# Third weight column rounded later, T1 in place of B12 in the classical columns, and another product order in the first Strassen pair

## The chip, the core and the metric

The kernel runs on one core of one Trainium2 chip. The metric is the device time of one execution in microseconds (us), as the median of several runs.

## What is computed

The reference is soft-capped attention followed by a mixture-of-experts style MLP with squared ReLU.

```
scores = cap * tanh(q @ k^T / sqrt(64) / cap);  attn = softmax(scores);  a = attn @ v
x = a, laid out as 1792 tokens x 768
h = maximum(x @ w_in, 0)          # w_in 768 x 2048
out = (h * h) @ w_out             # w_out 2048 x 768
```

There are 4 batches with 12 heads of 448 x 64. The weights come as 64-bit floats. TensorE multiplies rounded operands, and each operand is split into a high and a low part, so that a product of two matrices is three matmuls for each block (high x high, high x low, low x high).

## The kernel before

**Attention.** The main loop (from L615) runs over n, 24 pairs of heads, with two stages in flight: an iteration makes the scores of pair n on TensorE (PE, `scores` L410) and multiplies probabilities and v for pair n-1 (`pv_half` L454, `pv` L465, `sums` L472). ScalarE (ACT) does tanh and exp (L428, L436). VectorE (DVE) adds probabilities (L440, L445), inverts the sums of an older pair (L485), transposes the next k and q (L401), normalises an older pair into x (L509) and, last, empties the accumulators of pair n-1 from PSUM (`evac`, L478). In every iteration `evac` of pair n-1 has to be done before `pv_half` of pair n may write to the accumulators, since there is one such tile.

**Work slipped into attention.** Tables indexed by n put preparation for the MLP between these instructions. A weight column is 128 columns of w_in. Rounding it takes "size" (ACT, L40), "rest" (ACT, L43), "clip" (DVE L41), "shift" (L44), "sign" (L46) and "total" (L48). It is then split into high and low for each of its two halves (L572 and L574). `split_x_of` splits half of one 128-row block of x (L519, L520).

**First product.** x is cut into four blocks B11, B21, B12, B22 and w_in into 16 columns f. Columns 0 and 1 are computed classically, in half-products that accumulate two of the blocks each. The other 14 columns are seven pairs p, each a Strassen-Winograd scheme of seven products, numbered (m, p). A product is two halves j = 0, 1 of nine matmuls of 128 x 448 (`product`, L359). Both halves stand in one PSUM tile `hps` of shape [P, 2, 512], one bank per half. The products of a pair share tiles: product 6 adds into the tile seeded by product 1, is copied out as u (`keep_u`, L993, one ACT copy per half), and product 7 goes on adding into the same tile.

**Who sets the order.** In attention the order of each engine is that of the code. Behind it, a planner (`Plan`) holds tasks with costs, due times and dependencies and writes an order for every engine; PE follows the list `seq`. Waits between instructions are kept per tile, so a reader of a tile waits for its last writer.

**After the first product.** The squares are multiplied with w_out by another scheme (L1167), with operands that ACT and DVE split in time.

Of the kernel before, what the change touches and what calls it, by code (L numbers as in the profile page):

```python
# [240 lines left out]
def tile_softcap_attention_mlp(ctx, tc, q, k, v, cap, w_in, w_out, out):  # L241
# [359 lines left out]
    T1 = {24: ((0, 0), (1, 0), (2, 0)), 25: ((0, 1), (1, 1))}  # L601

# [5 lines left out]

    def half_unit(out, f, j, o):
        product(out, ops[f, o], xs[("B11", "B21")[o]], j, o == 0, o == 1)  # L610

# [3 lines left out]
    for n in range(NP + 1):  # L615
# [32 lines left out]
        if n == 1:  # L648
# [3 lines left out]
            nc.vector.memset(guard[top, 1:2], 0.0)  # L652
        if n - 6 in whole:
            split_x_of(n - 6)
# [27 lines left out]
    vector_work(NP + 1)  # L682
    half_unit(first[:, 0], 0, 0, 1)
    make_identity(nc, ident)
# [18 lines left out]
    plan = Plan(  # L703
        raw=[(0.0, i, p) for i, p in ((1, left), (2, right))],
        f=[(0.0, 0, left), (0.0, 1, right), (0.0, 3, right)],
        op=[], r=[(0.0, i) for i in range(2)], u=[(15.0, i) for i in range(3)],
        xf=[], xab=[], a=[(0.0, i) for i in range(NRAW)], ps=[(0.0, i) for i in range(2)],
        x=[(0.0, 0)],
    )

    def taken(room, *token):
        return SimpleNamespace(take=room, token=(0.0, *token))
# [6 lines left out]

    seq = [("u", 0, None), ("u", 1, None), ("u", 0, 0), ("u", 1, 0), (1, 1), ("u", 0, 1), (2, 1), ("u", 1, 1)]  # L720
    NEARLY = len(seq)
    for p in range(1, NFP):
        if p + 1 < NFP:
            seq += [(2, p)] * (p > 1) + [(m, p) for m in (6, 5, 7)] + [(1, p + 1), (4, p), (3, p)]
        else:
            seq += [(m, p) for m in (6, 5, 7, 2, 4, 3)]
    due, END = {}, 4.0
    for x in seq:
        due[x] = END
        END += STEP * (4 if x == seq[1] else 2)  # L730

# [32 lines left out]
    do("PE", 4.0, lambda: None, lag=0.0, due=-1.0)  # L764
    do("DVE", 4.4, lambda: None, lag=0.0, due=-1.0)
    spread_a = do("POOL", 0.7, lambda: spread(NP - 2), ready=5.5, lag=6.5)
# [56 lines left out]
    def round_column(first, f, at, early, raw=None):  # L823
# [12 lines left out]
        if raw:  # L836
            h.fetch, here = taken("raw", 0, left), None
        else:
            h.fetch, here = transfer("SP", fetch, 768, normal[2], due=at - 16.0, ready=at - early, take="raw")
# [26 lines left out]

    left_ops = {(1, "A11"): ready_op(2, 0), (1, "A12"): ready_op(2, 1)}
    columns = {(1, 0): SimpleNamespace(f=held[2], size=taken("f", 2, left), done=None)}
    raw3 = raws[3]

# [4 lines left out]
    def other_ops(p):  # L875
# [3 lines left out]
        at = due[6, p]  # L879
        o = left_ops[p, "A22"] = split_w(a22, at - 1.0, k.done)  # L880
        s1 = do("DVE", 0.56, lambda: nc.vector.tensor_add(out=a22(), in0=a21(), in1=a22()), k.done, o.lo, due=at - 4.0)
        s3 = less(a21, a11, a21, at - 3.5, s1, h.done)
# [17 lines left out]

    columns[1, 1] = round_column(True, 3, due[6, 1] - 5.0, 40.0, raw3)
    for p in range(1, NFP):
# [10 lines left out]
    x11, x21, x12, x22 = ([partial(x_of, a, b, c) for c in range(NHALF)] for a, b in ((0, 0), (0, 1), (1, 0), (1, 1)))  # L913
    at = due["u", 0, 0]
    d12 = [split_x("B12", c, [wide(x12[c])], at, [()], xg[2]) for c in range(NHALF)]
    d22 = [split_x("B22", c, [wide(x22[c])], due["u", 0, 1], [(normal[c],)], xg[0]) for c in range(NHALF)]
    at = due[6, 1] - 9.0
    t1 = [None] * (NHALF - 1) + [do("DVE", 0.62, lambda: t1_part(NHALF - 1, 1), due=at)]
    t3 = [minus(at + c + 0.4, x12[c], x22[c], x12[c], t1[c], *d12[c], normal[c]) for c in range(NHALF)]
    t2 = [minus(at + c + 0.7, x22[c], x22[c], x11[c], t3[c], *d22[c]) for c in range(NHALF)]  # L920
# [16 lines left out]

    def unit_task(key, j):

        _, f, o = key  # L940
        half = o is not None
        parts = [(("B12", "B22")[o], o)] if half else [("B11", 0), ("B21", 1)]

        def emit():
            if j == 0 and not o:
                new_bank("u", f, half)
            for b, k in parts:
                product(banks["u", f, half][:, j], ops[f, k], xs[b], j, k == 0, k == 1)

        need = [t for b, _ in parts for t in has_b[b][j]]  # L950
        return pe(key, emit, *need, cost=STEP * len(parts), take="ps" if j == 0 and not o else None)

# [57 lines left out]

    banks["u", 0, False] = first
    unit_ts = {}
    for key in seq[:NEARLY]:
        if key[0] != "u":
            strassen(*key)
            continue
        _, f, o = key
        ts = unit_ts[key] = [None if key == seq[0] and j == 0 else unit_task(key, j) for j in range(2)]
        half = o is not None
        if o != 0:  # L1020
            opens = unit_ts["u", f, 0 if half else None][0]
            out_u = relu_out(f, int(half), lambda f=f, half=half: banks["u", f, half], due[key], *ts)
            when(out_u, give=[opens or taken("ps", 2)])
        if half:
            when(ts[1], give=[ready_op(f, o).hi])
        if key == ("u", 1, 0):
            b12_read = ts
    d2 = [split_x("T2", c, [wide(x22[c])], due[6, 1] + 0.5 * c, [(t2[c],)], xg[1]) for c in range(NHALF)]
    d1 = [split_x("T1", c, [wide(x11[c])], due[5, 1] + 0.5 * c, [(t1[c], *b12_read)], xg[2]) for c in range(NHALF)]
    for c in range(NHALF):  # L1030
# [304 lines left out]
```

## Time and profile before

| quantity | value |
|---|---|
| median of 3 runs | 580.69 us (579.95 to 581.25) |
| the profiled execution itself | 580.98 us |
| its span, first to last instruction | 579.4 us |
| PE busy | 570.1 us, 98% of the span |
| DVE busy | 468.1 us, 81% |
| ACT busy | 374.7 us, 65% |
| granted TensorE clock | 1.00 of full speed |

A busy time is the union of an engine's instructions. Shares are averages over stages with different limits, so a stage has to be looked at by itself.

### The profile page before, as it was taken

What the parts mean: (1) busy time and instruction counts of PE and PEld (TensorE: products, weight loads), DVE (VectorE), ACT (ScalarE), POOL (GpSimd) and SP (SyncE); (2) the same over time, 40 slices, a digit from 0 to 9 for tenths busy, and PEclk for the clock granted to TensorE, in tenths of its full rate; (3) what the DMA queues carried; (4) which work ended last, traced back from release to release, by engine and by line L of the source; (5) the groups of instructions that cost most, each with busy time, mean ns of one, the idle gap of its engine ahead of it and who ended that gap; (6) DMA issues with size and microseconds to landing.
All of it is one profiled execution on the core that took longest, in us unless ns stands there. A gap on an engine that the chain in (4) does not pass through costs nothing.

```text
span 579.4 us, 10276 instructions
## 1 busy us (share of the span) xinstructions
PE 570.1 (98%) x3862; PEld 454.1 (78%) x3862; DVE 468.1 (81%) x603; ACT 374.7 (65%) x425; POOL 155.2 (27%) x245
## 2 busy tenths in 40 slices
PE   8999999999999999999999999999999999999997
PEld 5333333333369999998999999999999999999996
DVE  3778999999999999788698992756899996766661
ACT  5998999999946878587575873665535633323230
POOL 8788777877221001111120211100000000000000
PEclk9999999999999999999999999999999999999999
DMA  9999999997324837988889878995999236544511
GB/s 132 151 167 170 160 161 170 170 168 144 103 64 127 187 87 242 261 242 237 295 239 297 280 275 305 326 357 192 263 281 291 60 113 210 154 142 144 172 42 44
DMA packets 140728, 110.41 MB, mean 191 GB/s; under 512 B 55456, under 2 KB 129696, under 8 KB 140672
## 3 DMA queue, kind: packets, MB, share of 16 engines
q1 hardware_dynamic: 127136, 72.03, 51.7%
q0 software_dynamic: 12000, 37.39, 23.1%
q8 instruction: 31, 0.51, 0.4%
q10 hardware_dynamic: 1536, 0.27, 0.3%
q14 instruction: 25, 0.20, 0.1%
HBM read 82.84 MB, written 26.65 MB: 189 GB/s over the span
## 4 chain that ended last, share of the span: by engine, by line
PE 68%; issue 13%; DMA 8%; DVE 5%; POOL 3%; ACT 2%; SPq 0%; ACTq 0%; POOLq 0%; DVEq 0%
PE po L1167 35%; PE hps L359 18%; PE pv L465 6%; PE sc L410 5%; DMA kqn<-in_k_dram 2%; PE pv L454 2%; DMA wraw<-in_moe_w_in_dram 2%; DMA w_dram<-wf 1%; POOL kqn L370 1%; POOL g_dram L740 1%; PE pv L472 1%; ACT p L428 1%; PE sc L419 1%; DMA cap_sb<-in_cap_dram 1%; DMA kqn<-in_q_dram 1%
## 5 line engine op out<-in xcount | busy, mean ns | idle before, releaser
L1167 PE MATMUL po<-th,gh 128*128 128x384 f32 x728 | 189.8, 336 | 0.0
L1167 PEld LDWEIGHTS po<-th,gh 128*128 128x128 f32 x728 | 131.9, 188 | 0.0
L1167 PE MATMUL po<-th,gl 128*128 128x384 f32 x392 | 131.7, 336 | 0.0
L1156 ACT CAST gh<-a 128x1024 fp32r<-128x1024 f32 x47 | 49.4, 1051 | 97.5 <-PE po L1167 90.4
L359 PE MATMUL hps<-xt,op 128*128 128x448 f32 x450 | 92.4, 362 | 0.0
L359 PEld LDWEIGHTS hps<-xt,op 128*128 128x128 f32 x450 | 84.4, 187 | 5.6
L428 ACT ACTIVATE p<-sc 128x896 f32<-128x896 f32 x84 | 72.7, 908 | 8.2 <-PE sc L410 6.9
L1167 PEld LDWEIGHTS po<-th,gl 128*128 128x128 f32 x392 | 73.7, 188 | 0.0
L436 ACT ACTIVATE p<-p 128x1792 f32<-128x1792 f32 (+1 forms) x48 | 72.6, 1512 | 1.5
L1157 DVE TENSOR_TENSOR gl<-a,gh 128x1024 fp32r<-128x1024 f32 x47 | 57.5, 1224 | 19.3 <-ACT gh L1156 19.3
L359 PE MATMUL hps<-xs,op 128*128 128x448 f32 x324 | 67.6, 363 | 0.0
L359 PEld LDWEIGHTS hps<-xs,op 128*128 128x128 f32 x324 | 60.6, 187 | 4.7 <-issue 0.4
L370 POOL DMA_DIRECT2D kqn<-in_k_dram x92 | 58.3, 638 | 10.0 <-DVE kq L401 2.2
L410 PE MATMUL sc<-kq 64*64 64x448 f32 x576 | 60.4, 545 | 0.0
L465 PE MATMUL pv<-p,vn 128*32 128x448 f32 x576 | 59.1, 543 | 0.0
L359 PE MATMUL hps<-xh,op 128*128 128x448 f32 x168 | 49.6, 363 | 0.8 <-ACT u L993 0.8
L465 PEld LDWEIGHTS pv<-p,vn 128*32 128x32 f32 x576 | 16.2, 109 | 40.5 <-issue 40.5
L410 PEld LDWEIGHTS sc<-kq 64*64 64x64 f32 x576 | 20.2, 132 | 29.6 <-issue 22.7
L40 ACT ACTIVATE wf<-wraw 128x768 f32<-128x768 f32 x32 | 29.0, 907 | 16.3 <-DMA wraw<-in_moe_w_in_dram 7.8
L387 POOL DMA_DIRECT2D vn<-in_v_dram x48 | 35.2, 738 | 10.6 <-PE pv L465 4.7
L1180 DVE TENSOR_TENSOR osb<-s,po 128x384 f32<-128x384 f32 x27 | 14.9, 553 | 25.9 <-PE po L1167 25.8
L359 PEld LDWEIGHTS hps<-xh,op 128*128 128x128 f32 x168 | 31.5, 187 | 3.1 <-ACT u L993 1.1
(99 smaller groups left out, 807.4 us busy)
## 6 DMA issues: line engine op xcount, KB each, us to landing
a<-g_dram SPq DMA_DIRECT2D x56, 512.0 KB
wraw<-in_moe_w_out_dram SPq DMA_DIRECT2D x16, 768.0 KB
wraw<-in_moe_w_in_dram SPq DMA_DIRECT2D x24, 384.0 KB
g_dram<-r POOLq DMA_DIRECT2D x18, 448.0 KB, 4.5
g_dram<-u POOLq DMA_DIRECT2D x14, 448.0 KB, 4.8
w_dram<-wf POOLq DMA_DIRECT2D x16, 384.0 KB, 6.6
vn<-in_v_dram POOLq DMA_DIRECT2D x48, 112.0 KB, 5.7
kqn<-in_q_dram SPq DMA_DIRECT2D x93, 56.0 KB
```

The source lines that it names most:

```text
L40: size=lambda: nc.scalar.activation(out=magf, in_=high.bitcast(F32), func=ACTF.Abs, scale=2.0 ** 16),
L359: nc.tensor.matmul(out=out, lhsT=w, rhs=x[:, j], start=start and c == 0 and s == 0, stop=stop and c == NHALF - 1 and s == 2, skip_group_ch ...
L370: queue.dma_start(out=kqn[n % NKQ][32 * a:32 * a + 32, i], in_=x)
L387: nc.gpsimd.dma_start(out=vn[n % NKV][r, 1 + i:1 + i + NS], in_=x[i::2].rearrange("t r d -> r t d"))
L410: nc.tensor.matmul(out=sc[out, h, :S], lhsT=kt[r, keys(h, u)][:, out], rhs=qt[r], start=True, stop=True)
L428: nc.scalar.activation(out=p, in_=probs[n, u][:, :, :S], func=ACTF.Tanh, scale=by["qks"])
L436: nc.scalar.activation(out=p, in_=p, func=ACTF.Exp, scale=by["cap"])
L465: nc.tensor.matmul(out=pvs[n][quarter(i), h, :S], lhsT=vn[n % NKV][:, 1 + 3 * h + u, c], rhs=p[:, h], start=False, stop=(u == NU - 1), til ...
L1156: last["act"] = nc.scalar.copy(out=hi, in_=x)
L1157: last["dve"] = nc.vector.tensor_sub(out=lo, in0=x, in1=f32(hi))
L1167: last["mm"] = nc.tensor.matmul(out=po, lhsT=w[:, c], rhs=m[:, cols], start=(c == 0 and i == 0), stop=(c == HF - 1 and i == 2))
L1180: nc.vector.tensor_tensor(out=osb, in0=x, in1=y, op=op)
```

## The change

Three things are edited. The third weight column (f = 2) is not rounded within attention any more: its SCALAR and VECTOR entries are gone, and the planner rounds and splits it in the first product. The splits of x, one per iteration n = 6 to 17 before, stand where a table SPLIT says, and the high and low splits of columns 0 and 1 move to n = 22 and 23. The classical columns take another formula: the top half is B11 A0 + B21 A1 as before, and the bottom half is a copy of B11 A0, plus T1 A0, plus B22 A1, where T1 is a difference that the Strassen pairs need anyway; B12 is not split. The copy is made by ACT from PSUM to PSUM, in two halves, out of the top tile before B21 A1 is added to it. In the first pair, product 5 (which takes T1) goes ahead of 6 and 7.

```
-    SCALAR = {9: (0, "size"), 11: (0, "rest"), 15: (1, "size"), 17: (1, "rest"), 19: (2, "size"), 21: (2, "rest")}
-    VECTOR = {10: ((0, "clip"), (0, "shift")), 12: ((0, "sign"),), 14: ((0, "total"),), 16: ((0, "high0"), (0, "low0")),
-              18: ((0, "high1"), (0, "low1"), (1, "clip"), (1, "shift")), 19: ((1, "sign"),),
-              20: ((1, "total"), (1, "high0"), (1, "low0")), 21: ((1, "high1"), (1, "low1")),
-              22: ((2, "clip"), (2, "shift"), (2, "sign"), (2, "total")),
-              23: ((2, "high0"), (2, "low0"), (2, "high1"), (2, "low1"))}
+    SCALAR = {9: (0, "size"), 11: (0, "rest"), 15: (1, "size"), 17: (1, "rest")}
+    VECTOR = {10: ((0, "clip"), (0, "shift")), 12: ((0, "sign"),), 14: ((0, "total"),), 16: ((1, "clip"), (1, "shift")),
+              18: ((1, "sign"),), 20: ((1, "total"),),
+              22: ((0, "high0"), (0, "low0"), (0, "high1"), (0, "low1"), (1, "high0"), (1, "low0")),
+              23: ((1, "high1"), (1, "low1"))}
+    SPLIT = {6: (0,), 7: (1,), 8: (2,), 9: (3,), 10: (4,), 12: (6,), 14: (8,), 16: (10,), 19: (5,), 21: (7,), 23: (9, 11)}
...
+    UNIT = dict(a=(0, "B11"), b=(1, "B21"), t=(0, "T1"), c=(1, "B22"))
+
+    def half_unit(out, kind, f, j):
+
+        o, b = UNIT[kind]
+        product(out, ops[f, o], xs[b], j, kind == "a", kind in "bc")
...
         if n == NP:
             first = new_ps()
-            half_unit(first[:, 0], 0, 0, 0)
+            second = new_ps()
+            half_unit(first[:, 0], "a", 0, 0)
+            nc.scalar.copy(out=second[:, 0], in_=first[:, 0])
...
-    half_unit(first[:, 0], 0, 0, 1)
+    half_unit(first[:, 1], "a", 0, 1)
+    nc.scalar.copy(out=second[:, 1], in_=first[:, 1])
...
-    seq = [("u", 0, None), ("u", 1, None), ("u", 0, 0), ("u", 1, 0), (1, 1), ("u", 0, 1), (2, 1), ("u", 1, 1)]
+    seq = [("b", 0), ("a", 1), ("b", 1), ("t", 0), ("t", 1), (1, 1), ("c", 0), (2, 1), ("c", 1)]
...
-            seq += [(2, p)] * (p > 1) + [(m, p) for m in (6, 5, 7)] + [(1, p + 1), (4, p), (3, p)]
+            seq += [(2, p)] * (p > 1) + [(m, p) for m in ((5, 6, 7) if p == 1 else (6, 5, 7))] + [(1, p + 1), (4, p), (3, p)]
...
-    columns[1, 1] = round_column(True, 3, due[6, 1] - 5.0, 40.0, raw3)
+    columns[1, 0] = round_column(True, 2, due[1, 1] - 3.0, 40.0, raws[2])
+    for o in range(2):
+        first_op(1, o)
+    columns[1, 1] = round_column(True, 3, due[5, 1] - 3.0, 40.0, raws[3])
...
+        for j in range(2):
+            seeds[f].append(do("ACT", 0.55, partial(seed, j), ts[j], *seeds[f], due=due["b", f],
+                               take=None if j else "ps"))
```

The new line numbers are up to 16 higher than those before: L664 and L690 are the copies for column 0, L951 those for column 1, and L764, L753, L798, L862, L1009 are what L757, L746, L790, L854, L993 were.

**DVE at the end of attention.** These are the rows of the iterations n = 22 and 23 before, each ended by its L478; between them stand the rounding and the splits of column 2.

```order
L445 TENSOR_TENSOR add<-add,p 128x896
L485 RECIPROCAL cmp<-cmp 64x28
L41 TENSOR_SCALAR wf<-wf 128x768
L44 TENSOR_SCALAR wf<-wf 128x768
L46 SCALAR_TENSOR_TENSOR wf<-wraw,wf 128x768
L48 ISA wf<-wraw,wf 128x1536
L509 TENSOR_TENSOR xf<-u 128x448
L478 TENSOR_TENSOR u<-pv,guard 128x896
```

These are the rows of the changed kernel at the same place, from n = 22 on.

```order
L485 RECIPROCAL cmp<-cmp 64x28
L572 CAST op<-wf 128x384
L574 TENSOR_TENSOR op<-wf,op 128x384
...
L509 TENSOR_TENSOR xf<-u 128x448
L478 TENSOR_TENSOR u<-pv,guard 128x896
L440 TENSOR_TENSOR add<-p 128x896
L445 TENSOR_TENSOR add<-add,p 128x896
L485 RECIPROCAL cmp<-cmp 64x28
L519 CAST xs<-xf 128x448
L520 TENSOR_TENSOR xs<-xf,xs 128x448
```

In place of the rounding of column 2 there are three casts and subtractions of columns 0 and 1 in n = 22, and two splits of x and one more cast and subtraction in n = 23.

**ACT between attention and the first product.** Before, ACT ends its softmax work and then makes the casts of x.

```order
L436 ACTIVATE p<-p 128x896 [waits Activation_49]
...
L790 CAST xt<-xf 128x896 [waits PE_49]
L790 CAST xt<-xf 128x896
...
L43 ACTIVATE wraw<-wraw 128x768
L757 ACTIVATE r<-hps 128x896 [waits PE_49]
L746 ACTIVATE r<-r 128x896 [waits Activation_49]
```

In the changed kernel the copies between PSUM tiles stand there.

```order
L664 COPY hps<-hps 128x448 [waits PE_49]
L690 COPY hps<-hps 128x448 [waits PE_49,Activation_49]
...
L798 CAST xt<-xf 128x896 [waits DVE_49] x2
L40 ACTIVATE wf<-wraw 128x768 [waits DMAHW0_49]
L43 ACTIVATE wraw<-wraw 128x768
...
L764 ACTIVATE r<-hps 128x896 [waits PE_49]
L753 ACTIVATE r<-r 128x896 [waits Activation_49]
L951 COPY hps<-hps 128x448 [waits PE_49]
L798 CAST xt<-xf 128x896 [waits DVE_49]
L951 COPY hps<-hps 128x448 [waits PE_49,Activation_49]
```

PE has these rows at the start of the first product of the changed kernel, from the second half of B11 A0 on (hps_1952 is the top tile of column 0, hps_2071 that of column 1; xs_867 opens B21).

```order
L359 MATMUL hps_1952<-xs_632,op_1827 128x448 [waits Activation_49]
L359 MATMUL hps_1952<-xs_632,op_1827 128x448 x2
...
L359 MATMUL hps_1952<-xs_867,op_1830 128x448 [waits Activation_49]
L359 MATMUL hps_1952<-xs_867,op_1830 128x448 x2
...
L359 MATMUL hps_2071<-xs_632,op_1833 128x448 x3
...
L359 MATMUL hps_2071<-xs_786,op_1833 128x448 x3
L359 MATMUL hps_2071<-xs_867,op_1906 128x448 [waits Activation_49]
```

Before, the same products stand there with no wait on ACT. The L690 copy waits for the last matmul of the second half of B11 A0, and the first matmul of B21 A1 waits for it. The first L951 copy waits for the last matmul of the second half too, though it reads the first half, and the second one waits for the first half of B21 A1, which PE writes into the same tile.

**PE and ACT at products 6 and 7 of the first pair.** Before, PE goes from product 6 (tile hps_2244) to 5 (hps_2358) and back to the tile of 6 for product 7.

```order
L359 MATMUL hps_2244<-xt_2227,op_2246 128x448 x3
L359 MATMUL hps_2358<-xt_2212,op_2258 128x448 [waits Activation_49]
L359 MATMUL hps_2358<-xt_2212,op_2258 128x448 [waits DVE_49] x2
...
L359 MATMUL hps_2358<-xt_2215,op_2258 128x448 x3
L359 MATMUL hps_2358<-xt_2260,op_2258 128x448 x3
L359 MATMUL hps_2244<-xh_2292,op_2305 128x448 [waits Activation_49]
L359 MATMUL hps_2244<-xl_2351,op_2305 128x448 [waits DVE_49]
```

In the changed kernel product 5 (hps_2322) is first, and 6 and 7 follow each other in one tile, hps_2237.

```order
L359 MATMUL hps_2322<-xt_2050,op_2287 128x448 x3
L359 MATMUL hps_2237<-xt_2212,op_2283 128x448 x2
...
L359 MATMUL hps_2237<-xt_2250,op_2283 128x448 x3
L359 MATMUL hps_2237<-xt_2253,op_2283 128x448 x3
L359 MATMUL hps_2237<-xh_2235,op_2316 128x448 [waits Activation_49]
L359 MATMUL hps_2237<-xl_2362,op_2316 128x448 [waits DVE_49]
```

The first row of product 7 (operand op_2316) waits for the second of the two copies that ACT makes of product 6, and ACT has these rows there.

```order
L40 ACTIVATE wf_2364<-wraw_2170 128x768
L43 ACTIVATE wraw_2170<-wraw_2170 128x768
L1009 COPY u_2381<-hps_2237 128x448
L798 CAST xh_2385<-xf_895 128x896
L1009 COPY u_2381<-hps_2237 128x448
L798 CAST xh_2393<-u_2366 128x896
```

Product 5's eighteen matmuls no longer lie between the end of product 6 and the start of product 7, and a cast of 896 columns stands between the two copies.

## Rows read from the trace of the kernel before

**Rows 1.** The page, part 1: busy us, share, instructions of each engine.

```profile
PE 570.1 (98%) x3862; PEld 454.1 (78%) x3862; DVE 468.1 (81%) x603; ACT 374.7 (65%) x425; POOL 155.2 (27%) x245
```

**Rows 2.** Busy time of each engine by stretch (--windows; columns named in its head).

```profile
core 0: us, PE busy (x) PEld busy (x) DVE busy (x) ACT busy (x) POOL busy (x), PEclk, DMA share, GB/s
...
15.29:65.85 50.56, 50.56 (x544) 17.78 (x548) 41.84 (x53) 48.19 (x46) 40.21 (x62) 1.00 1.08 161
65.85:157.16 91.31, 90.08 (x957) 30.05 (x949) 87.44 (x121) 88.16 (x85) 66.81 (x102) 1.00 0.92 157
...
166.58:371.00 204.42, 203.64 (x1021) 190.54 (x1018) 174.64 (x250) 144.61 (x204) 33.06 (x55) 1.00 0.77 233
371.00:575.00 204.00, 204.00 (x1178) 203.82 (x1176) 150.48 (x152) 81.91 (x80) 0.54 (x1) 1.00 0.60 183
```

**Rows 3.** Timeline of PE, starts of L454 (n = 11, 23) and of the first product.

```profile
78.66 0.98 PE L454 MATMUL pv<-p,vn 64*64 64x448 f32 x8
...
157.16 0.98 PE L454 MATMUL pv<-p,vn 64*64 64x448 f32 x8 [0.35 <-ACT p L428]
...
166.58 12.88 PE L359 MATMUL hps<-xs,op 128*128 128x448 f32 x63
```

**Rows 4.** Timeline of DVE in attention: a split of x, and one whole iteration.

```profile
107.94 0.34 DVE L519 CAST xs<-xf 128x448 fp32r<-128x448 f32 x1
...
108.86 0.62 DVE L509 TENSOR_TENSOR xf<-u 128x448 f32<-128x448 f32 x1
...
142.70 1.09 DVE L478 TENSOR_TENSOR u<-pv,guard 128x896 f32<-128x896 f32 x1
...
146.14 1.04 DVE L401 STREAM_TRANSPOSE kq<-kqn 128x896 f32<-128x896 f32 x1
147.12 0.31 DVE L572 CAST op<-wf 128x384 fp32r<-128x384 f32 x1
...
147.94 0.62 DVE L509 TENSOR_TENSOR xf<-e 128x448 f32<-128x448 f32 x1
148.66 1.09 DVE L478 TENSOR_TENSOR e<-pv,guard 128x896 f32<-128x896 f32 x1
```

**Rows 5.** Groups of DVE instructions from 76 to 163 us: rounding steps.

```profile
L46 DVE SCALAR_TENSOR_TENSOR wf<-wraw,wf 128x768 uint32<-128x768 uint32 x3 | 2.8, 944 | 0.0
L48 DVE CUSTOM_DVE_ANT_0 wf<-wraw,wf 128x1536 uint16<-128x1536 uint16 x3 | 2.8, 941 | 0.1
...
L44 DVE TENSOR_SCALAR wf<-wf 128x768 uint32<-128x768 uint32 x3 | 1.7, 570 | 0.1
...
L41 DVE TENSOR_SCALAR wf<-wf 128x768 f32<-128x768 f32 x3 | 1.6, 533 | 0.0
```

**Rows 6.** Timeline of PE, then of ACT, around the end of product (6, 1).

```profile
203.89 1.16 PE L359 MATMUL hps<-xt,op 128*128 128x448 f32 x5
...
204.69 0.53 ACT L993 COPY u<-hps 128x448 f32<-128x448 f32 x1 [1.13 <-PE hps L359]
205.12 0.52 ACT L854 CAST op<-wf 128x384 fp32r<-128x384 f32 x1
...
207.64 0.95 ACT L790 CAST xh<-u 128x896 fp32r<-128x896 f32 x1
208.48 0.93 ACT L40 ACTIVATE wf<-wraw 128x768 f32<-128x768 f32 x1
```

**Rows 7.** Timeline of ACT, then of PE, around the one gap of PE.

```profile
265.27 0.89 ACT L40 ACTIVATE wf<-wraw 128x768 f32<-128x768 f32 x1 [2.45 <-DMA wraw<-in_moe_w_in_dram]
266.06 0.52 ACT L993 COPY u<-hps 128x448 f32<-128x448 f32 x1
...
262.09 3.77 PE L359 MATMUL hps<-xs,op 128*128 128x448 f32 x18
266.63 0.47 PE L359 MATMUL hps<-xh,op 128*128 128x448 f32 x1 [0.78 <-ACT u L993]
266.94 0.37 PE L359 MATMUL hps<-xl,op 128*128 128x448 f32 x1
```

More of the change, by code (lines that the diff above doesn't have):

```diff
@@ L652, in tile_softcap_attention_mlp @@
             nc.vector.memset(guard[top, 1:2], 0.0)
-        if n - 6 in whole:
-            split_x_of(n - 6)
+        for m in SPLIT.get(n, ()):
+            split_x_of(m)
         vector_work(n)
@@ L703, in tile_softcap_attention_mlp @@
     plan = Plan(
[L704 to L707, printed above, removed]
+        raw=[(0.0, 2, right)],
+        f=[(0.0, 0, left), (0.0, 1, right), (0.0, 2, left), (0.0, 3, right)],
+        op=[(0.0, i) for i in (4, 5)], r=[(0.0, i) for i in range(2)], u=[(15.0, i) for i in range(3)],
+        xf=[], xab=[], a=[(0.0, i) for i in range(NRAW)], ps=[(0.0, 0)],
         x=[(0.0, 0)],
@@ L729, in tile_softcap_attention_mlp @@
         due[x] = END
[L730 removed]
+        END += STEP * 2
     def transfer(engine, emit, kb, *after, due, give=(), **kw):
@@ L836, in round_column @@
         if raw:
-            h.fetch, here = taken("raw", 0, left), None
+            h.fetch, here = taken("raw", 3 - f, left), None
         else:
@@ L865, in ready_op @@
         return SimpleNamespace(t=ops[f, o], hi=taken("op", 2 * f + o), lo=None)
-    left_ops = {(1, "A11"): ready_op(2, 0), (1, "A12"): ready_op(2, 1)}
-    columns = {(1, 0): SimpleNamespace(f=held[2], size=taken("f", 2, left), done=None)}
-    raw3 = raws[3]
+    left_ops, columns = {}, {}
     def round_pair(p, e):
@@ L936, in new_bank, with seed_second, seed, unit_task @@
         banks[name] = (ps_x.tile([P, 2, 512], F32, tag="x", name="hps")[:, :, :S] if name[0] == "X" else new_ps())
[L938 to L942, printed above, removed]
-        def emit():
[L945 to L951, printed above, removed]
+    seeds = {}
+    def seed_second(f, ts):
+        def seed(j):
+            if j == 0:
+                new_bank("u", f, True)
+            nc.scalar.copy(out=banks["u", f, True][:, j], in_=banks["u", f, False][:, j])
+        seeds[f] = []
+        for j in range(2):
+            seeds[f].append(do("ACT", 0.55, partial(seed, j), ts[j], *seeds[f], due=due["b", f],
+                               take=None if j else "ps"))
+    def unit_task(kind, f, j):
+        b = UNIT[kind][1]
+        def emit():
+            if kind == "a" and j == 0:
+                new_bank("u", f, False)
+            half_unit(banks["u", f, kind in "tc"][:, j], kind, f, j)
+        copied = [seeds[f][j]] if kind in "bt" and f in seeds else []
+        return pe((kind, f), emit, *has_b[b][j], *copied, take="ps" if kind == "a" and j == 0 else None)
     USES = {1: ("A11", "B11", "X"), 2: ("A12", "B21", "X"), 3: ("S4", "B22", "V"), 4: ("A22", "T4", "Y"),
@@ L1009, in strassen @@
                 when(join, give=[bank_by["V", p]])
-    banks["u", 0, False] = first
-    unit_ts = {}
+    banks["u", 0, False], banks["u", 0, True] = first, second
+    bank_by["u", 0, False], bank_by["u", 0, True] = taken("ps", 1), taken("ps", 2)
     for key in seq[:NEARLY]:
-        if key[0] != "u":
+        if key[0] not in UNIT:
             strassen(*key)
             continue
[L1017 to L1021, printed above, removed]
-            out_u = relu_out(f, int(half), lambda f=f, half=half: banks["u", f, half], due[key], *ts)
[L1023 to L1027, printed above, removed]
+        kind, f = key
+        ts = [unit_task(kind, f, j) for j in range(2)]
+        if kind == "a":
+            seed_second(f, ts)
+            bank_by["u", f, False], bank_by["u", f, True] = ts[0], seeds[f][0]
+        if kind in "bc":
+            half = kind == "c"
+            out_u = relu_out(f, int(half), lambda f=f, half=half: banks["u", f, half], due[key], *ts)
+            when(out_u, give=[bank_by["u", f, half]])
+        if kind in "tc":
+            when(ts[1], give=[ready_op(f, UNIT[kind][0]).hi])
     d2 = [split_x("T2", c, [wide(x22[c])], due[6, 1] + 0.5 * c, [(t2[c],)], xg[1]) for c in range(NHALF)]
-    d1 = [split_x("T1", c, [wide(x11[c])], due[5, 1] + 0.5 * c, [(t1[c], *b12_read)], xg[2]) for c in range(NHALF)]
     for c in range(NHALF):
```

19 lines of the change are left out of this document (8 added, 11 removed).

## The prediction

> **What bounds the kernel now.** I read the busy shares first [rows 1]: PE is busy 98% of the span. By stretch [rows 2] it is busy without a break from 371 to 575 us, in the product with w_out, and 203.64 of 204.42 us in the first product. That stretch has one stop, 0.78 us [rows 7]. Nothing edited here lies in the product with w_out, so the change can act in attention and in the first product alone; in both, less work on DVE or ACT counts only where PE waits for it.
>
> Attention has two parts. From 15.29 to 65.85 (four pairs of iterations) PE is busy for all of it [rows 2]: 50.56 / 4 = 12.64 us a pair. From 65.85 to 157.16 (seven pairs) it takes 91.31 where 7 x 12.64 = 88.48, so something else paces it by 2.83 us. DVE is busy there for 87.44 of 91.31 and ACT for 88.16, with x splits and column rounding added. Which? An iteration of DVE from L478 to L478 is 148.66 - 142.70 = 5.96 us, of which one cast and subtraction are 147.94 - 147.12 = 0.82 [rows 4]. So the fixed part is 5.14, or 10.28 a pair, and 12.64 leaves 2.36 a pair for added work. The added pieces: an x split 108.86 - 107.94 = 0.92 [rows 4], clip with shift some 1.1, sign 0.94, total 0.94 [rows 5]. By the tables, each pair from n = 9, 10 to 21, 22 had between 2.6 and 2.9 of it, for example n = 13, 14 two splits and a total, 2.78, and n = 21, 22 one cast and subtraction plus a whole rounding, less the transpose that n = 22 no longer has (147.12 - 146.14 = 0.98 [rows 4]). Seven times the excess of about 0.4 is 2.8: DVE it is.
>
> **Attention after.** The pair n = 9, 10 keeps its load (two splits, clip and shift). From n = 11 to 20 each pair has at most one split and one or two pieces, under 2.1 and so below 2.36: PE paces them. L454 of n = 11 starts at 78.66 and that of n = 23 at 157.16 [rows 3]; six pairs at 12.64 end at 154.50, a gain of 2.66. Two deductions. First, n = 22 and 23 now carry three and one casts with subtractions (0.82 each) and two splits, less two transposes: 5.14 - 0.98 + 2.46 = 6.62, and 5.14 - 0.98 + 1.84 + 0.82 = 6.82 us. That is 13.44 against 12.64, 0.8 over. DVE starts this stretch ahead, since it has been waiting for PE: stepping the two engines through both iterations I am left with 0.25 of wait (bounds 0 and 0.8). Second, ACT: in 65.85 to 157.16 it is nearly as busy as DVE, and the three pairs from n = 11 on that keep a size or a rest step come out, by my count of its starts, within 0.1 of 12.64; I take 0.15 (bounds 0 and 0.5). **Attention: -2.66 + 0.25 + 0.15 = -2.26** (bounds -2.66 and -1.36). Removed ACT work (two rounding steps, three casts of x) and DVE work (column 2) is counted in that; what moves into the first product has cover: DVE is busy 174.64 of 204.42 there and ACT 144.61 [rows 2], and DVE starts it some 3 us ahead with three subtractions of x fewer. Stepping through the first 40 us of it, each operand is ready at least a microsecond before its product, column 3's fetch included. I cost this at nothing; without that microsecond, it would be a stop of up to 1 us at (5, 1).
>
> **The copies of the classical columns.** This is the new price. The copy is between B11 A0 and B21 A1, which follow each other directly in one tile: PE's first matmul of B21 A1 waits for ACT, and ACT for PE. For column 0 it is one stop (the second copy can only start when the second half is complete, and both copies hold back the first matmul). For column 1 the copies come after both halves, and the second copy waits for the first half of B21 A1 again, so there are two stops. The price of one is read from product (6, 1) [rows 6]. Its last matmul starts at 204.29 (the third start of the row at 203.89, in steps of 0.2; I count 188 matmuls from 166.58 [rows 3]) and the copy starts at 204.69, 0.40 later. ACT had been idle for 1.13 us before it, although the first half that it copies had started its last matmul nine steps, 1.8 us, before that: it waited for both halves. From copy start to restart PE takes 266.63 - 266.06 = 0.57, and the step after the restart is 0.31 for 0.2 [rows 7]. Sum: 0.40 + 0.57 + 0.11 - 0.20 that the next start would have taken anyway = 0.88. The copies here write PSUM for SBUF, 448 columns, which no row shows; I take the same 0.53. **Three stops: +2.64** (bounds 2.0, if a copy follows sooner, and 3.2, since before the second one ACT has casts, two rounding steps, a ReLU and a square queued, which my count has done only 0.25 us early).
>
> The Trainium skill, "PSUM — Partial Sum Buffer", section "PSUM bank collisions raise a hardware error", has it that PSUM needs to be guarded by bank (and quadrant), and by its section "Terms" one matmul output is at most one bank; so by that rule a copy of half 0 may run under the matmuls of half 1, and none of these stops is needed. The row at 204.69 shows this program waiting for the whole tile; by the row the term is +2.64, by the page it would be 0.
>
> **Products 5, 6, 7 of the first pair.** Before, product 5 (18 matmuls, 18 x 0.2 = 3.6 us) lay between 6 and 7 and hid the two copies of product 6. Now 7 follows 6 in the same tile and waits for the second copy, and between the two copies ACT has a cast of 896 columns. Last start of 6 to first copy 0.40; copy to next instruction 205.12 - 204.69 = 0.43; the cast 208.48 - 207.64 = 0.84 [rows 6]; second copy to restart 0.57, restart 0.11, less 0.20: **+2.15** (bounds 1.3, if the cast were not there, and 3, if the cast's input is late by a microsecond). Behind the second copy on ACT wait a cast for product 7's last block and a rounding; the 2 us that PE loses covers them.
>
> **The stop at 266.63.** A rounding step, L40, stood between the two copies of a product and waited 2.45 us for its weights [rows 7]: PE's last start before was 262.09 + 17 x 0.2 = 265.49, so the restart came 0.94 late, 1.05 with the slow step. In the changed order ACT's L40 there comes behind both copies; one stands between two copies only at a place with a whole product, 3.6 us, of cover. I take it as gone, **-1.05**, at two chances in three; other stops of the kind, up to 1.5 us, can appear as every transfer shifts.
>
> **Sum.** -2.26 + 2.64 + 2.15 - 1.05 = +1.48, on the profiled execution's 580.98 (span 579.4 and some 1.6 around it): 582.46. That execution is 0.29 above the median of the runs, 580.69, so the median should be **582.2**, 0.3% slower. A difference under 0.2%, 1.16 us here, can't be told from none.
>
> **Rivals.**
> *The copies hide.* If the halves were waited for separately, the first copy would run under the other half's matmuls at every place, and products 6 and 7 likewise: 580.69 - 2.26 - 1.05 = 577.4, faster. The 1.13 us of idle ACT in [rows 6] speaks against it, and so do the waits in the order of the changed kernel: 6 in 100.
> *Stops at the low end.* Copies start sooner (2.0 for the three), the cast does not stand in the way (1.3), and attention gives 2.66: -2.66 + 2.0 + 1.3 - 1.05 = -0.4, 580.3; halfway from there to the forecast is no measurable difference. The copy from PSUM to PSUM, never seen at this size, decides it. 24 in 100, with a few for a little faster.
> *The stop at 266 stays or another takes its place.* 583.2; a transfer that lands 2.45 us late is a matter of queues that this change shifts. Against it is the order. 24 in 100.
> *Attention gains nothing.* If ACT, busy 88.16 of 91.31 [rows 2], paced that part rather than DVE, removing DVE work would give no more than the two ACT steps, about 0.8 of the 2.26: 583.7. The pair sums of DVE match the excess better, so 8 in 100.
> *The forecast*, 581.4 to 583.0: 38 in 100.
>
> **The numbers.** The range takes in all but the copies that hide and the extremes of the stops: 580.1 to 584.4. The forecast and the two slower rivals, and a part of the low end, make slower by over 0.2% 0.64; the low end and the forecast's lower edge make no difference 0.26; the hidden copies and a little of the low end make faster 0.10.
>
> **What would show it.** In the profile after: L454 of n = 23 near 154.5 and the first product starting near 164.3; DVE with idle time from 80 to 150 us; three stops of PE of some 0.6 to 0.7 us released by the copies L690 and L951, at about 166, 174 and 177; a stop near 2 us before product (7, 1), released by L1009, near 208; none near 266. It would be wrong if PE ran through the copies, if DVE still had no idle time in attention, or if PE stopped for an operand of column 2 or 3 (L862, L865).

## Result: 0.8% slower, and later than the range

The changed kernel took 585.44 us (median of 6 executions, 584.25 to 588.18) and the kernel before 580.97 on the same occasions: a ratio of 1.008, 95% interval 1.0057 to 1.0103. The direction was as forecast, the size was not: 4.5 us in place of 1.5, and 1.0 us above the range. The profiled execution took 584.25 us (span 582.7, 3.3 over the span before), so part of the loss is not in its trace.

The page of the changed kernel, part 1, answers to [rows 1]: busy us, share, instructions.

```profile
PE 570.1 (98%) x3862; PEld 454.0 (78%) x3862; DVE 463.9 (80%) x598; ACT 375.0 (64%) x428; POOL 156.8 (27%) x245
```

PE does the same work in the same 570.1 us, and DVE has lost 4.2 us of it. So the 3.3 us are stops. The timeline of PE has them; in brackets stands the idle time ahead of a row and what ended it.

```profile
155.88 0.93 PE L454 MATMUL pv<-p,vn 64*64 64x448 f32 x8
...
162.10 0.98 PE L454 MATMUL pv<-p,vn 64*64 64x448 f32 x8 [0.51 <-DVE u L478]
...
165.79 2.08 PE L359 MATMUL hps<-xs,op 128*128 128x448 f32 x9
168.53 7.48 PE L359 MATMUL hps<-xs,op 128*128 128x448 f32 x36 [0.66 <-ACT hps L690]
176.62 2.08 PE L359 MATMUL hps<-xs,op 128*128 128x448 f32 x9 [0.61 <-ACT hps L951]
179.36 2.08 PE L359 MATMUL hps<-xs,op 128*128 128x448 f32 x9 [0.66 <-ACT hps L951]
212.41 0.47 PE L359 MATMUL hps<-xh,op 128*128 128x448 f32 x1 [1.89 <-ACT u L1009]
```

The four stops at copies are there, each at its place in the order of the products and near its size, and the stop at 266.63 [rows 7] is gone. Attention disappoints: L454 of n = 23 starts at 155.88, not 154.50, and the first product at 165.79, against 166.58 before [rows 3] and 164.3 by the forecast.

The table splits each profiled execution at the start of the first product (the first L359 after attention) and at the start of the product with w_out; the rows below "changed" are the experiments.

| kernel | first product starts | w_out starts | between |
|---|---|---|---|
| before | 166.58 | 371.15 | 204.57 |
| changed | 165.79 | 374.53 | 208.74 |
| changed, second trace | 165.97 | 376.36 | 210.39 |
| products 6, 5, 7 | 166.22 | 372.71 | 206.49 |
| copies covered | 164.56 | 371.09 | 206.53 |
| both | 166.32 | 370.30 | 203.98 |
| attention alone | 165.43 | 373.29 | 207.86 |
| T1 scheme alone | 167.53 | 376.67 | 209.14 |
| long stop | 165.85 | 378.34 | 212.49 |
| both, no v loads | 164.08 | 367.60 | 203.52 |
| before, no v loads | 166.31 | 369.82 | 203.51 |
| both, fetches spread | 164.33 | 367.98 | 203.65 |
| both, transpose first | 168.82 | 372.93 | 204.11 |
| both, inverse last | 166.24 | 372.03 | 205.79 |

Two questions follow. Are the stops at the copies all that the first product lost? And what became of 1.5 us of the attention gain?

### The profile page after: what moved, and what is told of

The parts are those of the page before. It is cut to its first block, busy times and chain, and to the rows that moved or that the text cites. A ratio compares the mean times of both kernels' runs of the same rounds, so it can differ in the third digit from the quotient of the medians.

```text
span 582.7 us, 10277 instructions
## 1 busy us (share of the span) xinstructions
PE 570.1 (98%) x3862; PEld 454.0 (78%) x3862; DVE 463.9 (80%) x598; ACT 375.0 (64%) x428; POOL 156.8 (27%) x245
## 4 chain that ended last, share of the span: by engine, by line
PE 72%; DMA 11%; DVE 7%; issue 3%; ACT 3%; POOL 2%; SPq 1%; ACTq 0%; DVEq 0%; POOLq 0%
PE po L1182 35%; PE hps L359 30%; PE pv L465 3%; DMA kqn<-in_k_dram 3%; DMA kqn<-in_q_dram 2%; PE sc L410 2%; DMA rd<-cmp 2%; DMA vn<-in_v_dram 2%; PE pv L454 1%; DMA wraw<-in_moe_w_in_dram 1%; POOL kqn L370 1%; DVE u L478 1%; DVE xf L509 1%; DVE kq L401 1%; DMA cap_sb<-in_cap_dram 1%
## 5 line engine op out<-in xcount | busy, mean ns | idle before, releaser
L359 PE MATMUL hps<-xt,op 128*128 128x448 f32 x450 | 92.4, 362 | 0.0
L359 PEld LDWEIGHTS hps<-xt,op 128*128 128x128 f32 x450 | 84.4, 187 | 5.6
L359 PE MATMUL hps<-xs,op 128*128 128x448 f32 x324 | 68.6, 364 | 1.9 <-ACT hps L951 1.3
L359 PEld LDWEIGHTS hps<-xs,op 128*128 128x128 f32 x324 | 60.3, 188 | 8.1 <-ACT hps L951 2.0
L359 PE MATMUL hps<-xh,op 128*128 128x448 f32 x168 | 49.5, 362 | 1.9 <-ACT u L1009 1.9
L48 DVE CUSTOM_DVE_ANT_0 wf<-wraw,wf 128x1536 uint16<-128x1536 uint16 x32 | 30.5, 953 | 5.6 <-ACT wraw L43 4.0
```

The source lines that it names most:

```text
L48: total=lambda: V.tensor_tensor(out=mag, in0=mag, in1=low, op=ALU.add),
```

## Experiments

### The stops at the copies: undone one by one

**Products 6, 5, 7 again.**

```
-[(m, p) for m in ((5, 6, 7) if p == 1 else (6, 5, 7))]
+[(m, p) for m in (6, 5, 7)]
```

> The changed kernel with products 6, 5, 7 in the first pair, as the other pairs have it; all else stays. Theory (stops at copies add up): the stop of 1.89 us before product (7, 1) goes, the three stops at the copies of the classical columns stay, span 582.7 - 2.15 = 580.6 us, time some 2.1 us under that of the changed kernel. Rival (another wait stands right behind that stop, an operand of product 7 or of column 3): the stop shrinks by less than 1 us and the time with it. On the clock: the changed kernel had a mean granted clock of 0.995 to 0.997 in three of six executions; if stops of PE bring that on, it is rarer here; if it has nothing to do with them, it comes in about half the executions of every kernel of this call, before included.

Measured: 582.48 us, 1.0031 of the kernel before (1.0018 to 1.0045). The stop before product (7, 1) is gone, the three others stay; the stretch between is 208.74 - 206.49 = 2.25 us shorter, for 2.15 expected. On the clock this run says nothing: its trace has the lower clock only behind PE's last matmul, where it costs nothing.

**The copies covered.** The half-products are put in an order in which another tile's product stands between a copy and the product that waits for it.

```
-seq = [("b", 0), ("a", 1), ("b", 1), ("t", 0), ("t", 1), (1, 1), ("c", 0), (2, 1), ("c", 1)]
+seq = [("a", 1), ("b", 0), ("t", 0), ("b", 1), ("t", 1), (1, 1), ("c", 0), (2, 1), ("c", 1)]
```

> The changed kernel with the half-products of the classical columns in the order a of column 1, b of 0, t of 0, b of 1, t of 1, so that a product of another tile lies between each copy and the product that waits for it; order 5, 6, 7 stays. Theory: the stops behind L951 go, that behind L690 too, the 1.89 us before product (7, 1) stays; span 582.7 - 2.64 = 580.1 us. Rival (the operands of T1 or the PSUM buffers are late in this order): one stop of 0.5 us or more at the first T1 product or at b of column 1 takes their place, span 581 or more. Clock as in the run before.

Measured: 582.44 us, 1.0028 (1.0017 to 1.0039). The profiled span was 579.4. The three stops are gone, and the stop before product (7, 1) stays, 1.90 us; a new one of 0.52 us behind the seed copy L998 appeared at 192.40, at another place than the rival had it. The stretch is 2.21 us shorter, new stop included. In this execution the first product started at 164.56, so attention gave nearly what was forecast (164.3), while the changed kernel's own trace, with the same attention, had it at 165.79: the gain of attention is not a constant.

**Both edits.**

> Both edits together: products 6, 5, 7 and the reordered classical columns. Theory (the delays add, 2.15 + 2.64): no stop of PE at a copy is left, span 582.7 - 4.79 = 577.9 us, time about 579.5, some 1.5 us below the kernel before, and a granted clock of 1.00 in all executions. Rival: the hidden time is taken by the next wait, span 579 or more; or the lower clock comes here just as often.

Measured: 579.72 us, 0.9983 (0.9972 to 0.9994), a little faster than before. No copy stops PE, and the stretch is 208.74 - 203.98 = 4.76 us shorter for 4.79 expected. The delays add. But its first product starts at 166.32, so nearly nothing is left of the attention gain here, and the span is 578.8 rather than 577.9.

**The T1 scheme alone**, with the attention tables of the kernel before.

> The changed kernel with the attention of the kernel before (third column rounded there, one split of x per iteration), so only the T1 scheme and products 5, 6, 7. Theory: attention ends where it did before, near 166.6 us; three stops at copies (2.6) and one before product (7, 1), now with a rounding step and a cast of 384 columns between the copies (2.15 + 0.4); span about 579.4 + 5.1 - 0.6 = 583.9, time 585.5. Rival (rounding column 2 in the first product, not the copies, carries a part of the loss): time 583.5 or less.

Measured: 586.18 us, 1.0094 (1.0079 to 1.0108). With the copies and without the edit of attention the kernel loses even more. The stretch between alone is 4.57 us longer than before (209.14 for 204.57), so the copies carry the loss and the rival falls. Attention did not end where it was expected: the first product starts at 167.53, 0.95 us later than in the trace of the kernel before, which has the same attention tables. The stop at product (7, 1) looks different here. These are rows of ACT, then of PE, from its timeline.

```profile
212.52 0.53 ACT L1008 COPY u<-hps 128x448 f32<-128x448 f32 x1 [1.53 <-PE hps L359]
...
215.22 0.53 ACT L1008 COPY u<-hps 128x448 f32<-128x448 f32 x1 [0.94 <-PE hps L359]
...
213.10 0.47 PE L359 MATMUL hps<-xh,op 128*128 128x448 f32 x1 [0.62 <-ACT u L1008]
...
215.81 0.47 PE L359 MATMUL hps<-xh,op 128*128 128x448 f32 x1 [0.62 <-ACT u L1008]
```

In this program the planner wrote the first half of product 7 ahead of the second copy. PE goes on after the first copy alone, then the second copy waits for PE, and PE for it: two stops of 0.62 in place of one of 1.89. The two halves are thus not tied to each other by the hardware; which waits exist follows from the order in which the program writes to and reads from a tile. That agrees with the Trainium skill, "PSUM — Partial Sum Buffer", section "PSUM bank collisions raise a hardware error", which asks for a guard by bank: here PE writes one bank of a tile whose other bank has still to be copied.

### Attention: what paces it after the change

In the trace of the changed kernel DVE has waits that it did not have before. These are DVE's waits from 60 to 165 us (engine, line, releaser: us in all, times, longest).

```profile
DVE cmp L485 <- DMA cmp<-u: 2.5, 2, 2.1
DVE u L478 <- PE pv L472: 1.2, 2, 0.7
DVE e L478 <- PE pv L472: 0.7, 1, 0.7
```

In the trace of the kernel before this view is empty from 60 to 165 us: DVE did not wait there. In that of the T1 scheme alone, with the same attention tables as before, L485 waits 0.7 us in all, in two places. Now L485, the inverse of the sums, waits for the small transfer that brings the sums (cmp). The longest wait, with DVE's rows around it, then PE's and SP's:

```profile
115.51 1.09 DVE L478 TENSOR_TENSOR u<-pv,guard 128x896 f32<-128x896 f32 x1
...
123.14 1.09 DVE L445 TENSOR_TENSOR add<-add,p 128x896 f32<-128x896 f32 x1
126.32 0.32 DVE L485 RECIPROCAL cmp<-cmp 64x28 f32<-64x28 f32 x1 [2.09 <-DMA cmp<-u]
...
129.31 1.09 DVE L478 TENSOR_TENSOR u<-pv,guard 128x896 f32<-128x896 f32 x1
...
130.55 0.98 PE L454 MATMUL pv<-p,vn 64*64 64x448 f32 x8 [0.59 <-DVE u L478]
...
113.94 3.16 SPq L370 DMA_DIRECT2D kqn<-in_q_dram  x4
117.42 1.58 SPq L585 DMA_DIRECT2D wraw<-in_moe_w_in_dram  x2
119.10 1.17 SPq L481 DMA_DIRECT2D cmp<-u  x2
```

L478 at 115.51 writes the sums and ends at 116.60. Their transfer is issued only at 119.10, since SP's queue first issues four loads of q and two weight fetches, and it takes until 126.32, 6 us after its second half was issued. The DMA engines are 0.91 busy from 65.85 to 157.16 us; that their load makes the transfer long is argued here, not shown. DVE, ready at 124.23, waits 2.09 us, its L478 is late, and PE stops for 0.59.

**Without the loads of v.** If transfers pace attention now, fewer of them must bring the gain back, and the kernel before must not care.

```
-        if prep:
+        if prep and not 9 <= n <= 20:
             load_v(n + 1)
```

> The kernel with products 6, 5, 7 and the reordered classical columns, without the loads of v for pairs 10 to 21 (the old v stays in its buffers, so the output for these pairs is not the reference's). It takes 24 transfers of 112 KB off the DMA engines in the second part of attention. Theory (with the lighter tables, attention is paced by transfers: DVE waits for the transfer of the sums and hands the wait on): L485 waits under 0.5 us in all, the first product starts near 164.3 in place of 166.3, time some 2 us under 579.7. Rival (DVE or ACT work paces it): it starts at 166, no gain.

> The control: the kernel before with the same loads of v left out (again not the reference's output for these pairs). Theory (before, the work of DVE paces attention and the transfers are hidden behind it): the first product starts near 166.6 as before, time 580.6 within 0.5. Rival (transfers paced it before as well, and the excess of 2.83 us came from them): it starts 1 to 2 us earlier, time 578.6 to 579.6.

Measured: 577.60 us with both edits, 0.9942 (0.9927 to 0.9957), and 579.62 for the kernel before, 0.9975 (0.9964 to 0.9986). The first rows of the first product, of the two in this order:

```profile
164.08 5.28 PE L359 MATMUL hps<-xs,op 128*128 128x448 f32 x25
```

```profile
166.31 2.88 PE L359 MATMUL hps<-xs,op 128*128 128x448 f32 x13
```

The same relief moves the changed attention by 2.24 us (from 166.32) and that of the kernel before by 0.27. So before, DVE's work was the pace in the main, as the prediction had it, and after it the transfers are. Single traces scatter by as much as 1.8 us, so the medians weigh more: 2.12 us less with both edits (579.72 to 577.60). The 1.25 us that the kernel before gains in time lie elsewhere: its stretch between is 203.51 for 204.57, so the stop at 266 is missing, 1.06 us.

**Spreading two fetches.** A smaller and complete remedy: the third column is not needed early any more, so its fetches need not come two in an iteration.

```
-    FETCH = 2, ..., 13, 14, 15, 15, 16, 16, 17, 21, 21, 22, 22, 23, 23
+    FETCH = 2, ..., 13, 15, 16, 17, 18, 19, 20, 21, 21, 22, 22, 23, 23
```

> The kernel with products 6, 5, 7 and the reordered classical columns, with the fetches of the third and fourth column spread: one in each of the iterations 15 to 20, then two each, in place of two each in 15 and 16 and none from 18 to 20. Theory (the wait of DVE near 126 us falls where two weight fetches stand in one iteration ahead of the transfer of the sums on SP's queue): the wait shrinks, time 578.5 to 579.5. Rival (the DMA engines are full all along, whatever the order): 579.7 as without the edit.

Measured: 578.63 us, 0.9960 (0.9946 to 0.9974), with no wait of L485 at all. The timeline of SP, DVE and PE at the same place:

```profile
112.01 2.43 SPq L370 DMA_DIRECT2D kqn<-in_q_dram  x4
114.94 0.68 SPq L585 DMA_DIRECT2D wraw<-in_moe_w_in_dram  x1
116.16 1.46 SPq L481 DMA_DIRECT2D cmp<-u  x2
...
115.04 1.09 DVE L478 TENSOR_TENSOR u<-pv,guard 128x896 f32<-128x896 f32 x1
...
122.74 1.09 DVE L445 TENSOR_TENSOR add<-add,p 128x896 f32<-128x896 f32 x1
123.75 0.31 DVE L485 RECIPROCAL cmp<-cmp 64x28 f32<-64x28 f32 x1
...
164.33 4.88 PE L359 MATMUL hps<-xs,op 128*128 128x448 f32 x23
```

The transfer is issued at 116.16, as soon as L478 is done, and L485 follows L445 without a pause. The first product starts at 164.33, the 164.3 of the prediction. One trace of another kernel started nearly as early with the fetches as they were (164.56), but the times bear the edit out: the slowest of the five executions (578.86) is just below the fastest of the twelve with both edits alone (578.87). This is the fastest complete kernel here.

**Moving the inverse on DVE.** Two kernels with both edits gave the transfer more time: one has the transpose ahead of the inverse, the other has the inverse behind the splits and rounding steps.

```
+        if 0 < n < NP - 2:
+            turn_kq(2 if n == 1 else n + 2)
         if 3 <= n <= NP:
             invert(n - 3)
-        if 0 < n < NP - 2:
-            turn_kq(2 if n == 1 else n + 2)
```

> The kernel with products 6, 5, 7 and the reordered classical columns, and in attention the transpose L401 goes ahead of the inverse L485 on DVE, so that the transfer of the sums has 1.05 us more to land. Theory (DVE waits for that transfer and hands the wait on to PE): the waits of L485, 1.4 to 2.5 us in all in the runs so far, shrink to under 1; the first product starts near 164.6 in place of 166.3, time 578.0 to 579.0. Rival (DVE or ACT work paces it, the wait was slack): no gain, time 579.7.

> As the run before, but the inverse goes behind the splits and the rounding steps of its iteration, and its transfer out behind the loads of k and q on SP's queue. Theory: the wait of L485 is gone nearly everywhere, and the first product starts by 164.6; time 577.8 to 578.8. Rival (the transfer out of the inverse now comes 3 us later behind four loads on the queue, and normalise L509 waits for it): new waits of L509, time 580 or more.

Measured: 581.53 us, 1.0018 (1.0009 to 1.0027), and 581.82, 1.0025 (1.0015 to 1.0035): some 2 us slower than without. Their traces lose the time in two different places, neither of them the one that was aimed at.

With the transpose first, L401 stands ahead of the inverse, and it waits for transfers early in attention: 10.6 us in all from 12 to 72 us, 6.9 of them for loads of k and q, against 2.5 with both edits alone. DVE passes a part of that on to PE. These are a row of DVE and one of PE.

```profile
58.89 1.11 DVE L401 STREAM_TRANSPOSE kq<-kqn 128x896 f32<-128x896 f32 x1 [1.52 <-DMA kqn<-in_q_dram]
...
62.90 0.98 PE L454 MATMUL pv<-p,vn 64*64 64x448 f32 x8 [1.41 <-DVE u L478]
```

L454 of n = 9 starts at 69.64 for 66.04 with both edits alone, 3.6 us later; from there on this attention is 1.1 us shorter. So neither theory nor rival held: L485 waits only 0.5 us, L509 waits 2.2 us in its place, and the time was lost before either.

With the inverse last, L485 does not wait at all from 60 to 166 us, but L509 waits 2.9 us for the transfer that spreads the inverse, and the first product starts at 166.24, as it did without the edit (166.32). The stretch between is 1.81 us longer. Rows of DVE, ACT and PE behind attention:

```profile
166.71 0.62 DVE L509 TENSOR_TENSOR xf<-e 128x448 f32<-128x448 f32 x1 [1.48 <-DMA e<-rd]
...
170.87 2.63 ACT L798 CAST xt<-xf 128x896 fp32r<-128x896 f32 x3 [1.94 <-DVE xf L526]
...
180.39 3.87 PE L359 MATMUL hps<-xs,op 128*128 128x448 f32 x18 [1.27 <-ACT hps L951]
```

L509 is late, so are DVE's differences of x behind it (L526), ACT's casts (169.38 without the edit), and at last ACT's copy L951, for which PE stops 1.27 us; a stop of 0.44 at 267.51 comes on top. The rival written for this kernel held: sums, inverse and the spreading of the inverse are one chain of transfers, an inverse that waits less starts later, and the end of the chain pays.

### Attention alone

The kernel before with the new tables of attention and the third column rounded by the planner, its classical columns and product order unchanged.

> The kernel before with only the edit of attention: the third column rounded by the planner, the splits of x by the new table; the classical columns with B12 and products 6, 5, 7 as before. Theory from the trace of the changed kernel (DVE, now earlier, waits for the small transfer of the sums, up to 2.1 us in one place): attention ends some 0.8 us earlier than before, not 2.3; time 579.1 to 580.2, by whether the stop of 0.78 us at 266 stays. Rival (the wait for that transfer was a chance of one execution): attention 2.3 us shorter, time 577.6 to 578.7. Second rival: rounding column 2 in the first product costs stops there, time 580.9 or more.

Measured: 582.79 us, 1.0031 (1.0019 to 1.0043), slower than before. The second rival held. Attention gives 1.15 us (165.43 for 166.58), and the first product loses 3.29. PE's rows at product (7, 1):

```profile
209.62 0.47 PE L359 MATMUL hps<-xl,op 128*128 128x448 f32 x1 [1.72 <-DVE xl L796]
209.93 0.57 PE L359 MATMUL hps<-xh,op 128*128 128x448 f32 x2
211.10 0.74 PE L359 MATMUL hps<-xl,op 128*128 128x448 f32 x1 [0.59 <-DVE xl L796]
211.63 0.95 PE L359 MATMUL hps<-xh,op 128*128 128x448 f32 x2
212.38 0.57 PE L359 MATMUL hps<-xl,op 128*128 128x448 f32 x1
```

DVE is late with the low parts of product 7's operand (L796), two stops of 2.3 us in all. DVE is busy without a break from 196 to 214 us there. The kernel with both edits has the same product order and rounds the same column in the first product, but splits no B12, and it has no such stop: with B12 still to be split, that rounding does not fit. The rows behind the second stop show something else: matmuls that start 0.37 apart for the usual 0.2. The granted clock is 0.50 there, 1.2 GHz in place of 2.4. Against the 203.51 to 203.65 that kernels without any stop need between, this one loses some 4.3 us: the 2.3 of the stops, and by my estimate most of the other 2.0 to the clock.

### The lower clock behind a long stop

**The changed kernel again**, unedited, for a second trace.

> The changed kernel once more, for a second trace. Theory (a stop of near 2 us can be followed by a stretch at the lower clock, in some executions): time 585.4; where the mean clock is 0.997 or lower, the slow matmuls stand right behind the stop before product (7, 1) and cost 1.5 to 2 us. The start of the first product moves from execution to execution between 164.5 and 166.5. Rival: the lower clock stands elsewhere.

Measured: 586.44 us, 1.0093 (1.0076 to 1.0111), the profiled execution 586.11. Its stretch between is 1.65 us longer than in the first trace. By windows of 1 us (columns as in [rows 2], granted clock third from the end):

```profile
213.00:214.00 1.00, 1.00 (x7) 0.93 (x6) 1.00 (x2) 1.00 (x2) 0.00 (x0) 0.97 0.00 0
214.00:215.00 1.00, 1.00 (x4) 0.92 (x3) 1.00 (x3) 1.00 (x2) 0.00 (x0) 0.50 0.00 0
215.00:216.00 1.00, 1.00 (x4) 0.88 (x4) 0.63 (x1) 0.07 (x1) 0.00 (x0) 0.50 0.00 0
216.00:217.00 1.00, 1.00 (x5) 0.88 (x4) 0.00 (x0) 0.00 (x0) 0.00 (x0) 0.50 0.00 0
217.00:218.00 1.00, 1.00 (x6) 0.92 (x5) 0.00 (x0) 0.00 (x0) 0.00 (x0) 0.82 0.00 0
```

PE restarts at 212.65 after the stop of 1.89 us, runs a good microsecond at full clock and then some 3.4 us at half. In the first trace the same stop of 1.89 us is followed by full clock:

```profile
212.00:214.00 2.00, 1.59 (x8) 1.50 (x9) 2.00 (x4) 2.00 (x4) 0.00 (x0) 1.00 0.02 7
214.00:216.00 2.00, 2.00 (x12) 1.88 (x11) 1.39 (x2) 0.82 (x2) 0.00 (x0) 1.00 0.00 0
```

So the theory holds, with the word "can": one stop of one program, two outcomes.

**A longer stop.**

```
                if j == 0:
                    h.u = new_u()
+                for _ in range(4 * (j == 1 and (m, p) == (6, 1))):
+                    nc.scalar.copy(out=h.u[:, 0], in_=bank_of("Y")[:, 0])
```

> The changed kernel with four more ACT copies of 448 columns between the two copies of product (6, 1) (the first half is copied again into the same place), so that the stop before product (7, 1) is longer by 4 x 0.43 = 1.7 us; nothing else changes. Theory A (a long stop of PE is followed by matmuls at the lower clock, which cost more than the stop): stop 3.6 us, the matmuls behind it at a granted clock of 0.50 for some us, time 1.7 + about 1.5 over the changed kernel, some 588.5. Theory B (the lower clock has nothing to do with the stop): 1.7 over it, some 587.

Measured: 588.60 us, 1.0143 (1.0128 to 1.0157). The stop is 4.0 us, and the matmuls behind it run at 0.50 again:

```profile
214.00:216.00 2.00, 1.37 (x5) 1.25 (x6) 1.05 (x3) 2.00 (x4) 0.00 (x0) 0.81 0.00 0
216.00:218.00 2.00, 2.00 (x7) 1.80 (x6) 0.54 (x1) 1.04 (x2) 0.00 (x0) 0.50 0.00 0
218.00:220.00 2.00, 2.00 (x10) 1.84 (x10) 0.00 (x0) 0.00 (x0) 0.00 (x0) 0.84 0.00 0
```

The stretch is 212.49 - 208.74 = 3.75 us longer than in the first trace of the changed kernel: 2.13 of longer stop (4.02 for 1.89), and 1.62 that go with the clock, as in the second trace. So theory A, by the trace: by time alone the run is 2.2 and 3.2 us over the two medians of the changed kernel (586.44 and 585.44), and in the first of these three of four executions have a mean clock of 0.995 already.

## Why the prediction was wrong

**The bound.** Right. PE is the bound outside attention, and in attention before, the work of DVE set the pace in the main: with half the loads of v gone that attention moved by 0.27 us only.

**Attention, -2.26: this step failed.** The text said of the pairs from n = 11 on that their DVE work is under what PE leaves, so PE paces them. DVE's work is under it, but L485 also needs the transfer of the sums, which in the trace of the kernel before had always landed when DVE came to it, because DVE was late. An earlier DVE meets it: waits of 2.5 us in all, a stop of PE of 0.59 at 130.55 and one of 0.24 at 79.21, and -0.79 us in the first trace, -0.61 in the second. Of the 1.47 that the first trace lacks, 0.31 is no effect of the tables: L454 of n = 9 already starts at 66.16 for 65.85, and the very first one at 15.60 for 15.29. The 0.51 at 162.10 is the wait that was priced at 0.25 for n = 22 and 23; it is 0.27 and 0.28 in the two kernels below, where L485 never waits. The two bounds, -2.66 and -1.36, came from DVE and ACT work alone, with no transfer in them, though the 0.92 of DMA share stood in [rows 2]. The size of the term was right as soon as nothing else stood in the way: 164.33 with two fetches spread, 164.08 without loads of v, for 164.3 expected. It varies by execution: seven traces with these tables and all loads as in the changed kernel started the first product between 164.56 and 166.32. All seven have L485 waiting near 126 us, for 1.09 to 2.09 us; the three that start last (165.97, 166.22 and 166.32) have a second wait near 132.5, of 0.33 to 0.57, and a stop of PE of 0.43 to 0.72 near 137 behind it. What makes the second wait come in some executions stays open.

**The copies, +2.64 and +2.15.** Right, in place, releaser and size: taking all four away gave 4.76 for 4.79. Three short stops of 0.61 to 0.66 and one of 1.89 were to be 0.6 to 0.7 and near 2.

**The stop at 266, -1.05.** Right: it is absent in the changed kernel, and three kernels without any stop need 203.51 to 203.65 between, 0.9 to 1.06 under the 204.57 of before. Yet it is no property of the order alone, as I argued: leaving out loads of v in the kernel before removed it as well, and with the inverse last a stop of 0.44 behind the same kind of copy came back at 267.51.

**Work moved at no cost.** Right for the changed kernel, where PE waits for no operand of columns 2 and 3. Attention alone shows how much of it hangs on the T1 scheme: with B12 to be split the same move costs 2.3 us of stops, and some 2 us more behind them.

**What was missing: the clock. This step failed too.** No term had a stop cost more than its own length; what follows a stop was put at nothing, without a reason. In the second trace the stop at product (7, 1) costs 1.65 us on top. Of the six executions of the changed kernel behind the result three had a mean granted clock of 1.00 and took 584.25, 584.39 and 585.12; the three at 0.995 to 0.997 took 585.77, 586.28 and 588.18. Of the four behind the second trace three had 0.995 and took 586.11 to 586.86, and one had 0.998 and took 585.71. The mean also counts the time after PE's last matmul, so it is only a hint for those without a trace; that all of them fell at this stop is argued from the second trace, not shown.

**Together.** First trace: -0.79 in attention and +4.17 between (4.79 - 1.05 = 3.74 forecast; the stops are each a little longer than priced, the rest was not traced) make the 3.3 of the span. With 1.65 in a part of the executions the median comes out 4.47 higher. Of the rivals on record none held; the nearest, attention that gains nothing, had the right size of the attention gain (0.8, measured 0.79) by luck: it named ACT, while the gain came back with fewer or later transfers and ACT's work as it was. That the kernel would be slower was no luck: the stops at the copies make it so in every trace that has all four.

## What to carry to other kernels

Before counting the gain of relieving an engine, follow each of its operands back to the transfer that brings it and ask when that lands; an engine that was late had hidden that time, and the next pacer may stand in a queue (here two weight fetches ahead of a 3.5 KB transfer). Where one engine has to copy a tile before another may go on in it, put another tile's work between: reordering two lists turned +0.8% into -0.2%, and spreading two fetches made it -0.4%. A stop of the matmul engine of near 2 us is, going by this kernel, to be priced with its own length and, for some executions, nearly as much again for the clock.

## What the runs showed of the hardware that was not expected

A stop of PE of 1.89 us was followed by 3.4 us at 1.2 GHz in one trace, at a cost of 1.65 us, and by full clock in another, as was one of 1.90 in the kernel with the copies covered; after 4.0 us, and after 1.72 and 0.59 close together, the half clock came as well, in the one trace that each has. Stops of 0.61 to 0.66 us, three of them within 11 us, left the clock at 1.00 in all five traces that have them, and so did single stops of 1.27 us (inverse last) and 1.41 us (transpose first). In the fourteen traces the clock fell nowhere else between 10 us and PE's last matmul. A transfer of 3.5 KB took about 6 us from its issue until the engine that waited for it went on, while the DMA engines were 0.9 busy.
